# Gated attention and hash-routed experts in one kernel: expert blocks of three sizes instead of two

## The chip, the cores and the metric

The kernel runs on one core of a Trainium2 chip. The metric is the device time of one execution in microseconds. One more execution was recorded by the hardware profiler; all views below are of it.

## The reference

Eight sequences of 2496 tokens go through a gated attention unit with squared ReLU, and every token then through one of eight experts, which its token id alone selects.

```python
scores = (1.0 / S) * np.matmul(z, z.transpose(0, 2, 1))     # z: 8 x 2496 x 64
attn = np.maximum(scores, 0.0) ** 2
x = (u * np.matmul(attn, v)).reshape(B * S, D)              # u, v: 8 x 2496 x 256
expert_idx = token_ids * np.int64(2654435761) % np.int64(E) # 19968 tokens, E = 8
for e in range(E):
    mask = expert_idx == e
    out[mask] = np.maximum(x[mask] @ w1[e], 0.0) @ w2[e]    # w1: 256 x 1024, w2: 1024 x 256
```

All is float32.

## The kernel before

**Attention.** The kernel walks over 200 steps: 8 batches `b`, 5 groups of queries `g` (256 queries of each half of the sequence, the last group 224), and 5 groups of keys `s` in the order `STEPS[g]`. A step is called `i`, its place in its group `pos`. The product of the scores with v is done by a seven-product scheme over 2x2 halves (halves of the sequence and of the 256 columns of v), so `attend` (L310) makes 7 products of 2 matmuls into four PSUM banks, which `acc_ps` holds once. `score` (L228 to L250) makes the scores of a pair of groups two steps ahead (`AHEAD`), on PE, ACT (ReLU, square) and DVE. Because the scores are symmetric, a pair is computed once: `mirror` (L272, DVE) turns it, `keep` (L281, L285, SP) writes it to DRAM, and `recall` (L289, ACT's queue) reads it back for the other group. `sums` (L261 to L264, DVE) makes four differences of the scores for the products. After the last step of a group `join` (L320 to L328) combines the seven products from PSUM into `o`; the first product of the next group writes into the same banks, so it waits for that. z of the next batch is loaded in four chunks (`load_z`, L158), turned by DVE (`turn_z`, L171) and copied to the lower partitions (`copy_z`, L176).

**From attention to slots.** `places` runs a piece per step from step 5 on. It works out on DVE, from the token ids, which slot of `x_slots` (in DRAM) each token has: tokens of one expert stand together, in blocks. A finished group goes through `gate` (DVE transposes of `o`), `put` (L349, SP, to DRAM), `fetch` (L357, L361, SP, back with tokens on partitions, and u with it through `load_u`, L206), `multiply` by u (L374, DVE) and `sort` (L395, four indirect stores by POOL). Groups whose slots are not known yet are kept back in the list `waiting` and fetched once `places` is done. The last group of all has `gate_late` instead: PE transposes (L384) and a multiply straight from PSUM (L386). The last batch has its columns in such an order that the first two blocks (`SURE = 2`) hold no token of its last three groups.

**Experts.** A block of 512 tokens (`NL` = 32 of them) belongs to one expert. It uses the seven-product scheme too, on weights prepared in `w_dram`: `up_large` (L901) and `down_large` (L931). What is left over of each expert's tokens goes into `NR` = 35 blocks of 128 with plain products: `up_small` (L954), `down_small` (L965). The last of an expert's blocks may be filled up with empty slots. Seven products come from `products` in the order 1, 6, 7, 5, 2, 3, 4, with a `yield` behind each; product 2 adds into the PSUM tile of 1, and 3 into that of 5. Product 3 must wait until DVE has read 5 (L872). Products 1 and 5 have tiles with the tag "held", the others "other"; D has one tile of "other", U two.

The order of all instructions is written out by hand (`manual_schedule`). For block `i` the loop at the end runs parts that yield, in turns given by a string: U and u are the up products of the 512 block and of its small blocks, D and d the down products of the block before, X and x the turns of the next block's rows on DVE (`turn_x`, L697 to L705), G the late gate. U yields 14 times, D 7 times, X twice. Weights and rows are loaded on SP at the end of a block's turn, rows and w1 (L717) for the block after the next, w2 for the next.

```python
ORDER = {"": "UuUDUuUDUdUDU" "XUDXUDUxUDUUDU", ...
         "first": "UUUUGUUGUUUUUUUU", "second": "DUDUUDUUDUUDUU" "xXUuDUXUuDUxUU"}
for j in at(i + 2):
    load_x(j)
for m in range(2):
    for j in at(i + 2 - m)[:2]:
        load_w(j, m)
```

Of the kernel before, what the change touches and what calls it, by code (L numbers as in the profile page):

```python
# [25 lines left out]
def kernel(  # L26
# [19 lines left out]
    P = 128  # L46
# [6 lines left out]
    BLK = 512  # L53
    TB = BLK // P
    NL = -(-(N - E * (BLK - 1)) // BLK)
    NR = (N - NL * BLK + E * (P - 1)) // P
    NB = NL + NR
    NS = NL * TB + NR
# [254 lines left out]
    def join(g, acc, home):  # L313

        w = queries(g)
        p = {m: acc[k][:, half, 0:w] for m, (k, half) in BANK.items()}
        o = home.tile([P, DP, 2, W], F32, name="o")
        r = opool.tile([P, 2, W], F32, name="r", bufs=1)
        p1, u2 = r[:, 0, 0:w], r[:, 1, 0:w]
        nc.scalar.copy(p1, p[1])  # L320
        c = lambda i, q: o[:, i, q, 0:w]
        nc.vector.tensor_add(c(0, 0), p1, p[2])  # L322
        nc.vector.tensor_add(u2, p1, p[6])
        nc.vector.tensor_add(c(0, 1), u2, p[5])
        nc.vector.tensor_add(c(0, 1), c(0, 1), p[3])
        nc.vector.tensor_add(u2, u2, p[7])
        nc.vector.tensor_add(c(1, 1), u2, p[5])
        nc.vector.tensor_sub(c(1, 0), u2, p[4])  # L328
        return o
# [46 lines left out]
    def gate_late(b, g, o):  # L376

        x_sb = late.tile([P, 2, 2, D], F32, name="x_row")
        for q in range(2):
            ps = down_ps.tile([P, 2, D], F32, name="g_ps", tag="any")  # L380
            for t in range(2):
                m = keys(g, t)
                for i in range(DP):
                    nc.tensor.transpose(ps[0:m, t, ts(i, P)], o[:, i, q, ds(t * P, m)], ident[:])  # L384
                x, y = times_u(b, g, x_sb, q, t, m)
                nc.vector.tensor_mul(x, ps[0:m, t].rearrange("p (h i k) -> p i h k", h=DP, k=L), y)  # L386
                sort(b, g, x_sb, 2 * q + t)
            yield
# [26 lines left out]
    def places():  # L415

        with tc.tile_pool(name="route", bufs=1) as route:
# [31 lines left out]
            def fill():  # L449
                if unfilled:  # L450
# [3 lines left out]
                        x_dram[ds(NL * BLK + c * P, n * P), :].rearrange("(c p) d -> p c d", p=P), zero[:].unsqueeze(1).to_broadcast([P, n, D]))  # L454
# [59 lines left out]
            upto = wpool.tile([P, E, C], F32, name="upto", tag="w")  # L514
# [10 lines left out]
            nc.vector.tensor_tensor_scan(upto[:].rearrange(flat_e), one[:].to_broadcast([P, E * C]), upto[:].rearrange(flat_e), 0.0,  # L525
                                         op0=OP.mult, op1=OP.add)
            yield
            nc.vector.tensor_add(rank[:], rank[:], upto[:])
# [22 lines left out]
            large, large_end = share(count, BLK, 0, NL, "large")  # L551
            in_large = route.tile([P, E], F32)
            nc.vector.tensor_scalar(in_large[:], large[:], float(BLK), None, op0=OP.mult)
            nc.vector.tensor_sub(count[:], count[:], in_large[:])
            small, small_end = share(count, P, P - 1, NR, "small")
# [3 lines left out]
            shift = route.tile([P, E], F32)  # L559
            nc.vector.tensor_sub(shift[:], large_end[:], large[:])  # L560
            nc.vector.scalar_tensor_tensor(shift[:], shift[:], float(BLK), first[:], op0=OP.mult, op1=OP.subtract)
            more = route.tile([P, E], F32)
            nc.vector.tensor_sub(more[:], small_end[:], small[:])
            nc.vector.tensor_scalar(more[:], more[:], float(P), float(NL * BLK), op0=OP.mult, op1=OP.add)
            nc.vector.tensor_add(first[:], first[:], in_large[:])
            nc.vector.tensor_sub(more[:], more[:], first[:])
            nc.vector.tensor_sub(more[:], more[:], shift[:])

            for end, b0, nb in ((large_end, 0, NL), (small_end, NL, NR)):
# [4 lines left out]
                eb = route.tile([1, max(NL, NR)], F32, name="eb")  # L576
# [9 lines left out]
            past = upto  # L586
            nc.vector.tensor_tensor(past[:], rank[:], each(first), op=OP.is_ge)
            yield
            nc.vector.tensor_mul(past[:], past[:], each(more))
            yield  # L590
            nc.vector.tensor_add(rank[:], rank[:], each(shift))
            yield
            nc.vector.tensor_add(rank[:], rank[:], past[:])
# [79 lines left out]
    def large(j):  # L673
        return j < NL

    def slot_tiles(j):
        return range(j * TB, (j + 1) * TB) if large(j) else range(NL * (TB - 1) + j, NL * (TB - 1) + j + 1)

    def load_x(j):
        n = len(slot_tiles(j)) * P  # L680
        xq[j] = gpool.tile([P, n // L, DP, L], F32, name="xq" if large(j) else "xqs")
# [4 lines left out]
    def turn_x(j):  # L686

        n = len(slot_tiles(j))
        if large(j):
            x = gpool.tile([P, 2, DP, 2 * P], F32, name="xT")  # L690
            t = gpool.tile([P, 4, 2 * P], F32, name="xs")
# [3 lines left out]
        m = min(2, n) * P // L  # L695
# [12 lines left out]
    def turn_x_at_once(j):  # L708
        for _ in turn_x(j):
            pass  # L710

    def load_w(j, m):

        e = nc.sync.value_load(eb_i[0:1, j:j + 1], min_val=0, max_val=E - 1)
        if large(j):
# [43 lines left out]
    routed, is_routed = places(), False  # L759
# [13 lines left out]
    for i, (b, g, s) in enumerate(steps):  # L773
# [6 lines left out]
        if b + 1 < B:  # L780
            for after, do in ((0, load_z), (5, turn_z), (6, copy_z)):
# [6 lines left out]
        if i >= len(steps) - SURE:  # L788
            turn_x_at_once(i - len(steps) + SURE)
        if pos == NT - 1:  # L790
            done = (b, g, join(g, acc, opool if i < len(steps) - 1 else late))
# [8 lines left out]
        if pos == 0 and done is not None:  # L800
# [19 lines left out]
        elif is_routed:  # L820
# [6 lines left out]
            if len(fetched) < 2 and waiting and (len(waiting) > 1 or i > put_at + (1 if i < len(steps) - NT else 0)):  # L827
                fetched.append((i, fetch(*waiting.pop(0))))
        if is_routed and 0 <= i - 32 < C:
# [7 lines left out]
        if i == len(steps) - 2:  # L837
            load_u(b, g, late)
            load_w(1, 0)
# [46 lines left out]
    def up_large(j):  # L886
# [3 lines left out]
        h = hpool.tile([P, 2, 2, FQ, 2 * P], F32, name="h")  # L890
        sums = hpool.tile([P, 3, FQ, 2 * P], F32, name="hs")
        hid[j] = h, sums
        take = {1: (0, y11), 2: (2, y21), 3: (6, y22), 4: (3, t4), 5: (4, t1), 6: (5, t2), 7: (1, t3)}
        for f in range(0, FQ, 2):
            def made(m, ps):
                first = ps is None
                if first:
                    ps = up_ps.tile([P, 2, 2 * P], F32, name="h_ps", tag="held" if m in (1, 5) else "other")
# [5 lines left out]
            r = rpool.tile([P, 2, 2, 2 * P], F32, name="r")  # L904
# [12 lines left out]
    def down_large(j):  # L917
        h, sums = hid[j]
        x11, x12, x21, x22 = (h[:, k, i] for i in range(2) for k in range(2))
# [3 lines left out]
        def made(m, ps):  # L923
            first = ps is None
            if first:
                held = m in (1, 5)
                ps = down_ps.tile([P, 2, P], F32, name="o_ps", tag="held" if held else "other", bufs=2 if held else 1)
            x, k = take[m]
            for t in range(2):
# [4 lines left out]
        r = rpool.tile([P, 2, 2, P], F32, name="ro")  # L934
        o = rpool.tile([P, TB, D], F32, name="o_sb")
        c = lambda i, k: o[:, ts(i, 2), ts(k, P)]

        def done(x, i, k, ps=None):
            if ps is not None:
                nc.scalar.copy(x, ps)  # L940
            elif i != k:
                for t in (2 * i, 2 * i + 1):
# [19 lines left out]
    def down_small(j):  # L962
        ps = down_ps.tile([P, D], F32, name="o_ps", tag="any")
        for f in range(FP):
# [10 lines left out]

    ORDER = {"": "UuUDUuUDUdUDU" "XUDXUDUxUDUUDU", "made": "UuUDUuUDUdUDU" "XUDXuUDUxuUDUUDU",
             "next": "UuUDUuUDUdUDU" "XUDXUDUxUDUUxDU", "last": "UdUDUuUDUuUDU" "XUDXUDdUxUDUUDU",
             "first": "UUUUGUUGUUUUUUUU", "second": "DUDUUDUUDUUDUU" "xXUuDUXUuDUxUU"}
# [3 lines left out]
    SMALL = [range(0)] + [range(*(NL + (k * NR + NL // 2) // (NL - 1) for k in (i, i + 1))) for i in range(NL - 1)]  # L982
# [69 lines left out]
```

## Time and profile before

| what | us |
|---|---|
| timed runs | 2510.62, 2514.37, 2514.39 (median 2514.37) |
| the profiled execution | 2507.8 |
| its span (first to last instruction) | 2506.0 |
| attention (to the end of the last `attend`) | 1453.9 |
| experts (from there to the last matmul) | 1043.8 |
| after the last matmul | 8.3 |

Views of the trace have one group of instructions per line: start, length, engine, line of the source, operation, what is written and read, shape, count, and in brackets how long the engine was idle before it and what ended that. A float32 matmul has two records, so `x16` is eight matmuls. The mean clock granted to TensorE was 0.998. PE is TensorE, PEld its weight loads, DVE VectorE, ACT ScalarE, POOL GpSimd, SP SyncE; `SPq` and the like are their queues for DMA.

### The profile page before, as it was taken

Reading aid. Unit: us, or ns where it says so; the run is one execution under the profiler, and the core shown is the slowest. Engines: PE = TensorE matmul, PEld = TensorE weight load, DVE = VectorE, ACT = ScalarE, POOL = GpSimd, SP = SyncE. Lnnn points to the kernel's source line nnn. Section 1 sums busy time; section 2 is a strip of 40 time slices with the busy share of each in tenths; the row PEclk is TensorE's granted clock in tenths of the full one; section 3 lists DMA queues with packets and bytes.
Section 4 is the critical chain, followed back from the end, with each engine's and each line's share of the span. In section 5 each row is a group of like instructions: output and inputs, shape, how many; then the busy total and the mean of one; then the engine's idle time right before and its main releaser. Section 6 shows DMA issues by size and latency. Waiting matters only on the chain.

```text
span 2506.0 us, 36968 instructions
## 1 busy us (share of the span) xinstructions
PE 2476.4 (99%) x13631; PEld 2110.9 (84%) x13631; DVE 1653.4 (66%) x3151; ACT 705.8 (28%) x1203; POOL 548.9 (22%) x532
## 2 busy tenths in 40 slices
PE   8999999999999999999999989999999999999998
PEld 6787787787787777877787889999999999999998
DVE  7798768768778677687687665545555555555553
ACT  4324324224223233133233112222222222222221
POOL 0000333322332233233223221111111111111112
PEclk9999999999999999999999999999999999999999
DMA  8776899798797897897888797766676667667762
GB/s 148 201 206 176 244 272 227 211 248 203 234 262 191 244 249 184 251 250 198 246 244 230 200 284 240 244 227 227 236 236 203 222 225 232 204 224 245 236 217 72
DMA packets 604661, 557.19 MB, mean 222 GB/s; under 512 B 287068, under 2 KB 544685, under 8 KB 594240
## 3 DMA queue, kind: packets, MB, share of 16 engines
q1 hardware_dynamic: 513984, 369.74, 54.6%
q10 hardware_dynamic: 63168, 97.86, 11.9%
q0 software_dynamic: 27328, 87.23, 10.0%
q8 instruction: 107, 1.75, 0.3%
q14 instruction: 74, 0.61, 0.1%
HBM read 375.55 MB, written 175.60 MB: 220 GB/s over the span
## 4 chain that ended last, share of the span: by engine, by line
PE 91%; DMA 5%; DVE 2%; issue 1%; SPq 0%; ACT 0%; POOL 0%; POOLq 0%; DVEq 0%; ACTq 0%
PE acc L310 42%; PE o_ps L931 16%; PE h_ps L901 15%; PE s_ps L228 8%; PE h_ps L954 5%; PE o_ps L965 5%; DMA a<-scores 3%; DMA u_sb<-in_u_dram 1%; DMA scores<-mirror 0%; DMA zn<-in_z_dram 0%; DVE x_row L374 0%; DVE t L261 0%; DVE t L262 0%; DVE t L263 0%; ACT a L242 0%
## 5 line engine op out<-in xcount | busy, mean ns | idle before, releaser
L242 ACT ACTIVATE a<-s_ps 128x512 f32<-128x512 f32 (+2 forms) x508 | 248.1, 579 | 736.5 <-PE s_ps L228 697.5
L310 PE MATMUL acc<-t,vc 128*128 128x256 f32 (+3 forms) x1600 | 402.6, 374 | 0.0
L310 PEld LDWEIGHTS acc<-a,v_sb 128*128 128x128 f32 (+1 forms) x1600 | 293.3, 190 | 125.0 <-issue 45.5
L310 PE MATMUL acc<-a,v_sb 128*128 128x256 f32 (+3 forms) x1600 | 382.6, 382 | 5.3 <-DVE o L322 5.2
L395 POOL DMA_INDIRECT x_slots<-x_row,row x160 | 192.3, 1202 | 849.7 <-DVE x_row L374 642.9
L310 PE MATMUL acc<-t,v_sb 128*128 128x256 f32 (+3 forms) x1600 | 369.7, 373 | 0.0
L310 PEld LDWEIGHTS acc<-t,vc 128*128 128x128 f32 (+1 forms) x1600 | 303.0, 190 | 34.5
L310 PEld LDWEIGHTS acc<-t,v_sb 128*128 128x128 f32 (+1 forms) x1600 | 303.5, 190 | 33.6
L261 DVE TENSOR_TENSOR t<-a 128x512 f32<-128x512 f32 (+1 forms) x200 | 134.5, 672 | 226.5 <-ACT a L250 162.0
L901 PE MATMUL h_ps<-xs,w 128*128 128x256 f32 x1024 | 258.1, 380 | 0.0
L931 PEld LDWEIGHTS o_ps<-w,h 128*128 128x128 f32 x2048 | 248.6, 192 | 6.5
L228 PE MATMUL s_ps<-zT 64*128 64x512 f32 (+1 forms) x960 | 241.4, 617 | 9.1 <-DVE zT L171 8.4
L931 PE MATMUL o_ps<-w,h 128*128 128x128 f32 x2048 | 249.3, 275 | 0.0
L908 ACT ACTIVATE h<-h 128x512 f32<-128x512 f32 x192 | 121.0, 630 | 349.1 <-DVE h L872 153.2
L854 POOL DMA_INDIRECT out_dram<-o_sb,idx x128 | 126.7, 990 | 420.8 <-ACT h L908 271.2
L272 DVE STREAM_TRANSPOSE mirror<-a 128x512 f32<-128x512 f32 x320 | 198.4, 677 | 6.6 <-DMA scores<-mirror 6.5
L310 PE MATMUL acc<-a,vc 128*128 128x256 f32 (+3 forms) x800 | 201.1, 374 | 0.0
L901 PE MATMUL h_ps<-xT,w 128*128 128x256 f32 x768 | 194.0, 382 | 1.2 <-DVE h L872 1.2
L901 PEld LDWEIGHTS h_ps<-xs,w 128*128 128x128 f32 x1024 | 178.5, 191 | 15.5
L931 PEld LDWEIGHTS o_ps<-w,hs 128*128 128x128 f32 x1536 | 186.4, 192 | 4.8
L931 PE MATMUL o_ps<-w,hs 128*128 128x128 f32 x1536 | 187.1, 275 | 0.0
L611 POOL DMA_INDIRECT slot_tokens<-token,addr x160 | 169.7, 1061 | 49.0 <-issue 48.1
(154 smaller groups left out, 2756.7 us busy)
## 6 DMA issues: line engine op xcount, KB each, us to landing
w<-w_blocks SPq DMA_DIRECT2D x64, 1792.0 KB, 11.3
scores<-mirror SPq DMA_DIRECT2D x276, 256.0 KB, 4.8
a<-scores ACTq DMA_DIRECT2D x48, 1024.0 KB, 5.8
w1s<-in_moe_w_dram SPq DMA_DIRECT2D x35, 1024.0 KB, 10.3
w2s<-in_moe_w_dram SPq DMA_DIRECT2D x35, 1024.0 KB, 11.5
a<-scores ACTq DMA_DIRECT2D x32, 896.0 KB, 7.3
w_blocks<-w POOLq DMA_DIRECT2D x16, 1792.0 KB, 8.1
u_sb<-in_u_dram SPq DMA_DIRECT2D x72, 256.0 KB, 5.2
```

The lines of the kernel that those rows point to most:

```text
L228: nc.tensor.matmul(to, z_h[:, ds(h * HS + s * W + j * P, P)], at, start=True, stop=True)
L242: nc.scalar.activation(to, at, AF.Relu, scale=1.0 / S)
L261: nc.vector.tensor_sub(t1, y12, y11)
L272: nc.vector.transpose(m[:, :, j, h].rearrange("p (n i) k -> p i n k", i=QB), a[:, j, h].rearrange("p (i t) q r -> p i (t q) r", t=2))
L310: nc.tensor.matmul(acc[k][:, half, 0:w], x[0:n, j, :], y[0:n, j], start=(first and j == 0 and half == 0), stop=(last and j == 1), skip_gro ...
L395: st = nc.gpsimd.indirect_dma_start(out=x_dram[:, :], out_offset=bass.IndirectOffsetOnAxis(ap=row[0:m, c:c + 1], axis=0), in_=x_sb[0:m, q, ...
L611: st = nc.gpsimd.indirect_dma_start(out=slot_dram[:, None], out_offset=bass.IndirectOffsetOnAxis(ap=addr[0:n, to:to + 1], axis=0), in_=tok ...
L854: st = nc.gpsimd.indirect_dma_start(out=out[:], out_offset=bass.IndirectOffsetOnAxis(ap=idx[:, col:col + 1], axis=0), in_=o, in_offset=Non ...
L901: nc.tensor.matmul(ps[:, r], w1[j][:, k, ts(f + r, P)], y, start=first and r == 0, stop=True, skip_group_check=True)
L931: nc.tensor.matmul(ps[:, t], x[:, f, ts(t, P)], w2_block(w2[j], k)[:, f], start=first and t == 0 and f == 0, stop=f == FQ - 1, skip_group_ ...
L954: nc.tensor.matmul(ps[:, i, :], w1[j][:, c, ts(f + i, P)], x[:, 0, c, 0:P], start=(c == 0), stop=(c == DP - 1))
L965: nc.tensor.matmul(ps[:], hid[j][:, f], w2[j][:, f, :], start=(f == 0), stop=(f == FP - 1))
```

## The change

**Three sizes of block.** Between the 512 blocks and the 128 blocks there are now `NM` = 7 blocks of 256, always full, which use the same seven-product code on halves of 128 (`up_big`, `down_big`: U products 128 columns wide, D products half as many matmuls). `NR` falls from 35 to 21; the number of slots stays 163 x 128. `places` works with three levels instead of two, which makes it four steps longer. Every fifth block of the large ones is a 256 block; a small block goes with a 512 block, at most one each, none with a 256 block or with the first two; the last block has one, whose down product comes last of all.

**Order.** The turns X of the next block move: the first from the start of the second half of the string into the first half, ahead of D's second product, the second from behind one U and D to near the end. The special orders for two smalls go.

**Seam.** The last two groups now both use PE transposes (`gate_at_once`): all eight first, then the four multiplies. For group 3 of the last batch this stands at step 196 and replaces gate, put and fetch; its `join` writes `o` in another order of columns (`turned_back`). For the last group it stands in block 0, with both PSUM tiles at once, and its sorts come after block 0's products. The first two blocks' turns come at steps 197 and 198 instead of 198 and 199, u of group 3 is loaded at step 194 and u of the last group at 196 (before 197 and 198).

**Attention.** `load_z` comes two steps sooner. A fetch comes at the earliest four steps after the one before it.

```diff
+    BLK, MID = 512, 256
+    TB, TM = BLK // P, MID // P
     NL = -(-(N - E * (BLK - 1)) // BLK)
-    NR = (N - NL * BLK + E * (P - 1)) // P
+    NM = -(-(N - NL * BLK - E * (MID - 1)) // MID)
+    NR = (N - NL * BLK - NM * MID + E * (P - 1)) // P
...
+    def gate_at_once(b, g, o, x_sb, bank):
+        made = []
         for q in range(2):
-            ps = down_ps.tile([P, 2, D], F32, name="g_ps", tag="any")
+            made.append(bank())
+            for t in range(2):
+                for i in range(DP):
+                    nc.tensor.transpose(made[q][0:keys(g, t), t, ts(i, P)], o[:, i, q, ds(t * P, keys(g, t))], ident[:])
+        yield
+        for q in range(2):
             for t in range(2):
                 m = keys(g, t)
-                for i in range(DP):
-                    nc.tensor.transpose(ps[0:m, t, ts(i, P)], o[:, i, q, ds(t * P, m)], ident[:])
                 x, y = times_u(b, g, x_sb, q, t, m)
-                nc.vector.tensor_mul(x, ps[0:m, t].rearrange("p (h i k) -> p i h k", h=DP, k=L), y)
-                sort(b, g, x_sb, 2 * q + t)
-            yield
+                nc.vector.tensor_mul(x, made[q][0:m, t].rearrange("p (h i k) -> p i h k", h=DP, k=L), y)
...
-            past = upto
-            nc.vector.tensor_tensor(past[:], rank[:], each(first), op=OP.is_ge)
...
+            for past, (lowest, more, _) in ((past_mid, levels[1]), (upto, levels[2])):
+                nc.vector.tensor_tensor(past, rank[:], each(lowest), op=OP.is_ge)
+                yield
+                nc.vector.tensor_mul(past, past, each(more))
+                yield
...
-            for after, do in ((0, load_z), (5, turn_z), (6, copy_z)):
+            for after, do in ((-2, load_z), (5, turn_z), (6, copy_z)):
...
-        if i >= len(steps) - SURE:
-            turn_x_at_once(i - len(steps) + SURE)
+        if i == len(steps) - 4:
+            x_sb = rowpool.tile([P, 2, 2, D], F32, name="x_row", bufs=3)
+            for _ in gate_at_once(*done, x_sb, lambda: mm_ps.tile([P, 2, D], F32, name="g_ps", tag="mm")):
+                pass
+            to_sort += [(*done[:2], x_sb, k) for k in range(4)]
+        if 0 <= i - (len(steps) - 3) < SURE:
+            for _ in turn_x(i - (len(steps) - 3)):
+                pass
...
-            if len(fetched) < 2 and waiting and (len(waiting) > 1 or i > put_at + (1 if i < len(steps) - NT else 0)):
+            if len(fetched) < 2 and waiting and i >= fetch_at + 4 and (len(waiting) > 1 or i > put_at + 1):
                 fetched.append((i, fetch(*waiting.pop(0))))
+                fetch_at = i
...
         if i == len(steps) - 2:
-            load_u(b, g, late)
             load_w(1, 0)
+        if i == len(steps) - NT - 1:
+            load_u(b, g)
+        if i == len(steps) - 4:
+            load_u(b, g, late)
...
-    ORDER = {"": "UuUDUuUDUdUDU" "XUDXUDUxUDUUDU", "made": "UuUDUuUDUdUDU" "XUDXuUDUxuUDUUDU",
-             "next": "UuUDUuUDUdUDU" "XUDXUDUxUDUUxDU", "last": "UdUDUuUDUuUDU" "XUDXUDdUxUDUUDU",
-             "first": "UUUUGUUGUUUUUUUU", "second": "DUDUUDUUDUUDUU" "xXUuDUXUuDUxUU"}
+    ORDER = {"first": "UUUUGUUUGUUUUUUU", "second": "DUDUDUUDUUDUU" "XUxUDUXUDUUUU",
+             "other": "UuUDUuUXDUdUDU" "UDUDUxUDUXUDU", "end": "DDDDDDDd"}
...
+    for i in range(NBIG):
+        BIG.append(mid.pop(0) if i % (NBIG // NM) == NBIG // NM - 1 and mid else large.pop(0))
+        SMALL.append([])
+    for behind in (True, False):
+        for i in range(NBIG - 1, 1, -1):
+            if small and BIG[i] < NL and (BIG[i - 1] >= NL) == behind and (behind or i % 2 == 0 or len(small) == 1):
+                SMALL[i].append(small.pop())
```

## The prediction

> **What bounds the kernel now.** First the page's busy times, then its chain.
>
> ```profile
> PE 2476.4 (99%) x13631; PEld 2110.9 (84%) x13631; DVE 1653.4 (66%) x3151; ACT 705.8 (28%) x1203; POOL 548.9 (22%) x532
> ...
> PE 91%; DMA 5%; DVE 2%; issue 1%; SPq 0%; ACT 0%; POOL 0%; POOLq 0%; DVEq 0%; ACTq 0%
> ```
>
> TensorE is never far from busy, and the chain runs through it. Busy time of matmuls is modelled, so I took prices from starts in PE's timeline, here inside the expert blocks (start, length, group):
>
> ```profile
> 1579.52 3.62 PE L965 MATMUL o_ps<-w2s,h 128*128 128x256 f32 x16
> 1582.97 1.03 PE L901 MATMUL h_ps<-xT,w 128*128 128x256 f32 x4
> 1583.84 1.95 PE L931 MATMUL o_ps<-w,h 128*128 128x128 f32 x16
> 1585.62 1.03 PE L901 MATMUL h_ps<-xs,w 128*128 128x256 f32 x4
> ...
> 1589.14 1.95 PE L954 MATMUL h_ps<-xTs,w1s 128*128 128x128 f32 x16
> 1590.92 1.03 PE L901 MATMUL h_ps<-xs,w 128*128 128x256 f32 x4
> ```
>
> A group ends where the next starts. One matmul of the program is two records. So a U product of a 512 block (L901) costs 0.865 us, a D product (L931) 1.787, half a small up (L954) 1.785, a small down (L965) 3.45. A record with 128 columns costs 1.787/16 = 0.112, one with 256 0.216. Then PE in three stages (length, PE busy, PEld, DVE, ACT, POOL, clock, DMA share, GB/s):
>
> ```profile
> 1247.00:1427.00 180.00, 179.81 (x826) 141.97 (x822) 135.47 (x266) 57.52 (x95) 57.97 (x52) 1.00 0.83 228
> 1427.00:1462.00 35.00, 30.77 (x162) 29.71 (x158) 22.36 (x48) 3.33 (x7) 7.03 (x7) 1.00 0.90 230
> 1600.00:2480.00 880.00, 880.00 (x6006) 827.96 (x6005) 463.29 (x837) 209.41 (x387) 138.11 (x141) 1.00 0.67 221
> ```
>
> The expert stage has no gap at all in 880 us: only less PE work can shorten it. All of PE's idle time lies elsewhere; reading PE's timeline right through gives 8.4 us at the start, 0.68 in routing, 5.2 in eight places of attention, 7.1 at the seam, and 8.3 after the last matmul. The seam and one of the eight:
>
> ```profile
> 381.08 1.99 PE L310 MATMUL acc<-a,v_sb 128*128 128x256 f32 x8 [1.92 <-DVE o L322]
> ...
> 1453.93 1.03 PE L901 MATMUL h_ps<-xT,w 128*128 128x256 f32 x4
> 1462.48 0.51 PE L384 MATMUL g_ps<-ident,o 128*96 128x128 f32 x2 [4.71 <-DVE x_row L386]
> 1462.78 3.53 PE L901 MATMUL h_ps<-xT,w 128*128 128x256 f32 x8
> 1467.43 0.42 PE L384 MATMUL g_ps<-ident,o 128*96 128x128 f32 x2 [0.90 <-DVE x_row L386]
> 1474.21 1.13 PE L901 MATMUL h_ps<-xT,w 128*128 128x256 f32 x4 [1.18 <-DVE h L872]
> 1476.04 1.95 PE L931 MATMUL o_ps<-w,h 128*128 128x128 f32 x16
> ```
>
> **What the Trainium skill says.** "Perfetto Trace Analysis", Identifying the Most-Contended Engine: matmul occupancy is a poor measure of headroom, LDWEIGHTS busy a better one. The trace agrees: PEld is 828 of 880 us (94%) in the expert stage against 79% in attention (142 of 180), so no slack is hidden there. "TensorE: Matmul & The Clock Gate", Part 1: the HAM clock gate: after an idle window of about 3.4 us the array runs at half clock until it has been busy as long. The trace agrees: after 4.71 us of idling two products took 3.37 us (1462.78 to 1466.15) instead of 1.73; after 1.18 us none slowed. The same page's specification table: VectorE's queue is strictly first in, first out. Agreed: at 368 DVE sat 11.96 us for a<-scores, and the join (L322) that PE waited for at 381 stood behind. "DMA: Bandwidth & Descriptors", Issuing engines are not separate DMA queues: all queues share 16 engines. Agreed: SP's keeps (L281) waited 388.8 us for landings of ACT's a<-scores.
>
> **The change part by part.**
>
> *Blocks.* 32+35 blocks become 32 of 512, 7 of 256 and 21 of 128. A small costs 2x1.785+3.45 = 7.02 us of PE. A middle block has 14 U products of 4 records (0.447) and 7 D products of 8 (0.894): 6.26+6.26 = 12.5 us, where two smalls cost 14.0. Seven times 1.52: **-10.6 us**, all on the bounding engine. DMA falls too: 3.5 MB of weights for a middle block, 4 MB for two smalls. DVE gets more: 18 operations of about 0.42 us, 5 of 0.28 and a turn of 2.0, some 11 us, against 2.2 for two smalls; 62 us in a stage where DVE is 53% busy.
>
> *Turns (X) inside a block's sequence.* What they can delay is D's second product: its o_ps has one buffer, so D's third product waits until DVE has read the second, and X's two transposes (1.30 us) now stand ahead of that read. I walked each kind of cycle from the PE end of U's fourth product. Block 512 after a middle one: DVE's c22 ends at 0.2+0.69 = 0.89, X at 2.2, the read (0.28) at 2.5; PE arrives at 0.89+2x0.865 = 2.62. Fits by 0.1. Block 512 after 512: read done 2.62, PE at 3.52. Middle block after 512 without a small behind it (three cycles): DVE still has the previous block's sums, read done about 1.2+1.79, PE about 0.35 sooner. Near misses elsewhere: I take **+1.5 us** in all, bounds 0 and +8 (0.2 in each of 39 cycles). X needs its x rows landed: they are issued almost a cycle before (the turn at 1493.98 used loads issued at 1474.7; landing takes at most 16.9), so I cost this at nothing; the shortest cycle, 18.8 us, needs 5 MB of weights and rows, 13 us at the 390 to 450 GB/s seen after 1500. Were that cover gone, it would be the rival below.
>
> *Seam.* Group 3 of the last batch loses put, fetch and their SP issues; eight PE transposes at 0.224 come instead: +1.8. Its DVE multiplies need u, issued right behind u of group 2 (which ended DVE's wait at 1443); DVE reaches them at about 1446. The last group's transposes come at once in two buffers, so the waits of 4.71 and 0.90 and the half clock after the first (1.64) go. What is late next: the second half of block 0. From PE's end of U's seventh product DVE needs 0.9 for the subtraction, 1.5 for four multiplies, 2.5 for four sums, 2.26 up to c22: 7.2 us; PE arrives after 5x0.865 = 4.3. Stall 2.9 instead of 1.18, too short for the clock gate. From 1453.93 to the first D took 22.1; now 14x0.865+8x0.22+2.9 = 16.8. With +1.8, and the 0.34 us at 1494 gone: **-3.8 us**, bounds -6 and +2. The last sorts start about 9.5 us into the block, and their landing gates SP's x of block 2: landed near 28, turned at 33. w2 of block 0 waited for none of them (issued at 1457.9) and is due at 16.8: cover of about 2 us.
>
> *Attention.* Fetches: before, the backlog was drained in steps 24 to 39; now one every 4 steps from 28 to 104, then the same steps as before. Each moves a 0.5 MB x_row and 0.5 MB of u on SP. z: 8 issues a batch pass two steps of keeps, so the turns of z (DVE waited 32.8 us for zn, 11 times) have seven steps instead of five. The waits that reach PE total 5.2 us. They can vanish, or others come, since DMA is already 83 to 86% busy: I take **-2**, bounds -5 and +5. Routing is four steps longer (three more 1.45 us operations and some 20 short ones on DVE, 6 us); it lies in steps where DVE is 83% busy and PE lost 0.7 us; cost nothing, at worst +6.
>
> *End.* A small down now ends the program. Before, POOL still had four stores of 1.28 us after the last D. Now these lie beside the small's 3.45 us; copy 0.4, store 1.3, landing 3.9 follow, about 6.3 against 8.3. D's third product directly behind the second stalls 0.67. **-1.3**, bounds -2.5 and +1.
>
> Sum: -10.6+1.5-3.8-2-1.3 = **-16.2 us**. The profiled execution took 2507.8 (span 2506.0), below all three timed runs (median 2514.4); carried to the median: **2498.2 us**, 0.64% less. A measurement of this kernel tells about 0.2%, 5 us, from no change.
>
> **Rivals.**
> 1. *The moved turn sets D's pace* (slower than before). If the transposes wait for xq, or DVE's backlog is a little larger than walked, every cycle pays at D's third product. From 16.2/39 = 0.42 us a cycle (beyond my 1.5 us) the gain is gone; a full exposed turn, 1.3 us, would give +35: 2530. For it: margins of 0.1 us. Against: DVE 47% idle, x issued early. Chance 0.09 slower, 0.14 for a part of it (2502 to 2512).
> 2. *Attention pays for the fetches.* A backlog kept to step 104 puts x and u transfers beside recalls and mirrors in three batches instead of one. At +5 instead of -2: 2505. Chance 0.12.
> 3. *Everything hides.* No new stall among blocks, attention's waits gone: -10.6-4.5-5.2-1.5 = -22: 2492. Chance 0.12.
> 4. *The middle blocks do not pay*: if 128 columns cost a middle block's U more than L954's, say 0.6 instead of 0.447, 7x14x0.15 = 15 us are lost and the time stays about 2513. LDWEIGHTS at 94% speaks for it; L931 and L954 already run this shape at 0.112 a record, against it. Chance 0.03.
>
> My forecast has 0.5. Range 2489 to 2509: from rival 3 with a run's scatter to most of rivals 1 (part) and 2. Faster by over 0.2% 0.86, within 0.05, slower 0.09.
>
> **What would show it.** Right: L954's and L965's successors with 672 and 336 records; middle U products 0.45 us apart; PE without gaps among blocks except tenths of a us before D's third product; one gap of about 3 us at the seam, waiting for c22, at full clock; about 6 us after the last matmul. Wrong: repeated gaps of 0.4 us or more on h_ps or o_ps matmuls, DVE waiting for xq<-x_slots, PE waiting for w<-w_blocks, or joins late by more than 5 us in all.

## The result, and the profile after

| | before | after |
|---|---|---|
| median of 20 runs (lowest to highest), us | 2513.05 (2508.93 to 2516.10) | 2517.60 (2513.78 to 2524.72) |
| profiled execution; its span, us | 2507.8; 2506.0 | 2517.7; 2515.9 |
| mean granted clock of TensorE | 0.998 | 0.996 |
| start of block 0's first product | 1453.93 | 1477.80 |
| from there to the first D | 22.1 | 20.3 |
| from the first D to the last matmul's end | 1021.7 | 1011.7 |
| after the last matmul | 8.3 | 6.2 |

A matmul's end is taken here as the start of its last record plus the price of one. The ratio of the medians is 1.0024, with a 95% interval from 1.0016 to 1.0031: the change makes the kernel slower by 0.24%, where 0.64% less was forecast. The table already tells where. The experts and the end give 12.1 us, block 0 another 1.8, and attention takes 23.9. The three add up to the spans' difference of 9.9 to within a tenth.

The page of the kernel after, its busy times and its chain, answers the first two lines of the prediction:

```profile
PE 2477.2 (98%) x13751; PEld 2113.6 (84%) x13751; DVE 1715.0 (68%) x3346; ACT 724.0 (29%) x1259; POOL 556.7 (22%) x532
...
PE 85%; DMA 7%; DVE 4%; issue 2%; SPq 1%; ACT 0%; ACTq 0%; POOL 0%; POOLq 0%; another core or an unknown queue 0%; DVEq 0%
```

PE's busy time did not fall although the blocks need less of it, and its share of the chain fell from 91% to 85%: the chain now leaves PE for DMA, DVE and queues. Busy time hides this, because slowed matmuls count as busy too. The expert stage of the kernel after (stretch, length, then PE, PEld, DVE, ACT, POOL, clock, DMA share, GB/s):

```profile
1498.00:2510.00 1012.00, 1011.32 (x7114) 956.73 (x7112) 594.01 (x1148) 259.11 (x502) 162.16 (x162) 1.00 0.67 220
```

There is as little idle time among the blocks as before, and the stage ends 10 us sooner after its start. PE's timeline of the kernel after, at the seam, in a middle block and at the end:

```profile
1477.80 1.03 PE L929 MATMUL h_ps<-xT,w 128*128 128x256 f32 x4
...
1481.26 1.23 PE L386 MATMUL g_ps<-ident,o 128*128 128x128 f32 x8
...
1494.72 2.08 PE L929 MATMUL h_ps<-xT,w 128*128 128x256 f32 x4 [4.04 <-DVE h L899]
1496.59 1.64 PE L929 MATMUL h_ps<-xs,w 128*128 128x256 f32 x4
1498.07 1.95 PE L960 MATMUL o_ps<-w,h 128*128 128x128 f32 x16
...
1596.62 0.61 PE L929 MATMUL h_ps<-xs,w 128*128 128x128 f32 x4
1597.06 1.95 PE L960 MATMUL o_ps<-w,h 128*128 128x128 f32 x16
...
1608.17 1.05 PE L960 MATMUL o_ps<-w,h 128*128 128x128 f32 x8
1609.06 1.03 PE L929 MATMUL h_ps<-xs,w 128*128 128x256 f32 x4
...
2497.25 2.05 PE L960 MATMUL o_ps<-w,h 128*128 128x128 f32 x16 [0.58 <-DVE ro L893]
...
2506.28 3.62 PE L994 MATMUL o_ps<-w2s,h 128*128 128x256 f32 x16
```

A middle block's U product takes 0.44 us and its D product 0.89, as forecast (0.447 and 0.894). Eight transposes are eight records and take 1.06 us (1481.26 to 1482.32). The seam's long gap waits for c22 (what L899 finishes, and U's third product waits for), as forecast, but is 4.04 us and not 2.9, and half clock follows it: two products in 3.35 us.

Some of the gaps of attention in the kernel after:

```profile
169.65 3.01 PE L312 MATMUL acc<-a,v_sb 128*128 128x224 f32 x8 [2.13 <-DVE o L325]
...
318.36 1.99 PE L312 MATMUL acc<-a,v_sb 128*128 128x256 f32 x8 [2.04 <-issue]
...
380.25 4.27 PE L230 MATMUL s_ps<-zT 64*128 64x512 f32 x8 [4.04 <-ACT a L244]
...
1302.51 3.08 PE L312 MATMUL acc<-a,v_sb 128*128 128x256 f32 x8 [2.32 <-DVE o L325]
```

Most are first products of a group that wait for the join. In all, PE stands idle 18.2 us in 13 places of attention, where it was 5.2 in seven (the prediction counted eight). Slow matmuls come on top: 3.01 us for what takes 1.78, 4.27 and 3.08 for 1.99. By the profile's granted clock, 17.1 us of attention ran at half clock (3.41 us each from 170.03, 688.86 and 1303.26, and 6.83 from 378.25), and none of attention before (the first 13 us of each kernel apart); PE was busy for 15.1 of them, so they cost about 7.5 us. The 13.0 us of further idling, 7.5 of half clock and 1.1 of transposes make up 21.6 of the 23.9.

What DVE waited for before and after (engine, line, what it waited for: us in total, times, longest):

```profile
DVE t L261 <- DMA a<-scores: 52.7, 17, 12.0
DVE zT L171 <- DMA zn<-in_z_dram: 37.7, 11, 5.2
```

```profile
DVE t L263 <- DMA a<-scores: 96.4, 29, 15.0
...
DVE zT L173 <- DMA zn<-in_z_dram: 5.0, 2, 3.9
```

The wait for z went from 37.7 to 5.0 us, as an earlier load should do. But 43.7 us more of waiting for recalled scores came in its place (96.4 for 52.7). Waits of DVE reach PE only in small part: before, there were 90 us of these two, and PE was idle for 5.2.

### The profile page after: what moved, and what is told of

The parts are those of the page before. It is cut to its first block, busy times and chain, and to the rows that moved or that the text cites. A ratio compares the mean times of both kernels' runs of the same rounds, so it can differ in the third digit from the quotient of the medians.

```text
span 2515.9 us, 37295 instructions
## 1 busy us (share of the span) xinstructions
PE 2477.2 (98%) x13751; PEld 2113.6 (84%) x13751; DVE 1715.0 (68%) x3346; ACT 724.0 (29%) x1259; POOL 556.7 (22%) x532
## 3 DMA queue, kind: packets, MB, share of 16 engines
q10 hardware_dynamic: 63168, 97.86, 12.1%
## 4 chain that ended last, share of the span: by engine, by line
PE 85%; DMA 7%; DVE 4%; issue 2%; SPq 1%; ACT 0%; ACTq 0%; POOL 0%; POOLq 0%; another core or an unknown queue 0%; DVEq 0%
PE acc L312 37%; PE o_ps L960 17%; PE h_ps L929 17%; PE s_ps L230 8%; DMA a<-scores 4%; PE h_ps L983 3%; PE o_ps L994 3%; DMA scores<-mirror 2%; DMA u_sb<-in_u_dram 1%; DVE t L263 1%; DMA v_sb<-in_v_dram 1%; DVE t L265 1%; DVE t L264 1%; SPq L283 0%; ACT a L244 0%
## 5 line engine op out<-in xcount | busy, mean ns | idle before, releaser
L929 PE MATMUL h_ps<-xs,w 128*128 128x256 f32 (+1 forms) x1248 | 288.7, 361 | 0.1
L881 POOL DMA_INDIRECT out_dram<-o_sb,idx x142 | 143.4, 1010 | 630.9 <-issue 419.3
L960 PEld LDWEIGHTS o_ps<-w,h 128*128 128x128 f32 x2272 | 275.7, 192 | 7.8 <-DVE ro L893 1.1
L960 PE MATMUL o_ps<-w,h 128*128 128x128 f32 x2272 | 279.3, 275 | 0.6 <-DVE ro L893 0.6
L230 PE MATMUL s_ps<-zT 64*128 64x512 f32 (+1 forms) x960 | 245.7, 622 | 13.9 <-DVE zT L173 8.6
L936 ACT ACTIVATE h<-h 128x512 f32<-128x512 f32 (+1 forms) x234 | 138.6, 592 | 356.9 <-DVE h L899 138.3
L929 PEld LDWEIGHTS h_ps<-xs,w 128*128 128x128 f32 x1248 | 208.5, 191 | 17.0 <-issue 0.5
L929 PE MATMUL h_ps<-xT,w 128*128 128x256 f32 (+1 forms) x936 | 215.1, 362 | 4.4 <-DVE h L899 4.0
L960 PEld LDWEIGHTS o_ps<-w,hs 128*128 128x128 f32 x1704 | 206.9, 192 | 4.9
L960 PE MATMUL o_ps<-w,hs 128*128 128x128 f32 x1704 | 209.3, 275 | 0.0
L626 POOL DMA_INDIRECT slot_tokens<-token,addr x160 | 175.2, 1095 | 65.4 <-issue 47.5
```

The costliest lines, as they stand in the source:

```text
L230: nc.tensor.matmul(to, z_h[:, ds(h * HS + s * W + j * P, P)], at, start=True, stop=True)
L626: st = nc.gpsimd.indirect_dma_start(out=slot_dram[:, None], out_offset=bass.IndirectOffsetOnAxis(ap=addr[0:n, to:to + 1], axis=0), in_=tok ...
L881: st = nc.gpsimd.indirect_dma_start(out=out[:], out_offset=bass.IndirectOffsetOnAxis(ap=idx[:, col:col + 1], axis=0), in_=o, in_offset=Non ...
L929: nc.tensor.matmul(ps[:, r], w1[j][:, k, ts(f + r, P)], y, start=first and r == 0, stop=True, skip_group_check=True)
L936: lambda o, i, k, ps=None: nc.scalar.activation(o, o if ps is None else ps, AF.Relu))
L960: nc.tensor.matmul(ps[:, t], x[:, f, ts(t, P)], w2_block(w2[j], k)[:, f], start=first and t == 0 and f == 0, stop=f == FQ - 1, skip_group_ ...
```

## The experiments

Every kernel computes all of the result. Each ratio is against runs of the kernel before on the same chip. For the experiments the medians of these were 2510.25 (e1 to e4), 2512.21 (r1 to r3 and e5), 2508.56 (g1 to g3 and x1) and 2507.98 us (h1 to h4), so ratios are compared, not medians. A hundredth of a per cent is 0.25 us. "Attention" is the start of block 0's first product in the one profiled execution.

| kernel | ratio (95%) | attention, us |
|---|---|---|
| before | 1 | 1453.9 |
| after | 1.0024 (1.0016 to 1.0031) | 1477.8 |
| e1_after_z_back | 1.0023 (1.0012 to 1.0033) | 1473.9 |
| e2_after_fetch_back | 1.0000 (0.9990 to 1.0011) | 1472.1 |
| e3_after_both_back | 0.9995 (0.9987 to 1.0003) | 1469.8 |
| e4_before_z_sooner | 1.0032 (1.0016 to 1.0048) | 1461.4 |
| e5_before_fetch_4 | 1.0048 (1.0030 to 1.0065) | 1470.9 |
| r1_before_routing_at_9 | 1.0063 (1.0045 to 1.0081) | 1472.5 |
| r2_both_back_routing_at_1 | 0.9946 (0.9929 to 0.9962) | 1461.5 |
| r3_after_routing_at_1 | 1.0040 (1.0031 to 1.0050) | 1475.6 |
| g1_before_fetch_4_on_pool | 1.0028 (1.0018 to 1.0039) | 1455.7 |
| g2_routing_at_1_fetch_on_pool | 0.9922 (0.9908 to 0.9936) | 1450.0 |
| g3_after_fetch_on_pool | 0.9974 (0.9965 to 0.9984) | 1470.9 |
| x1_turns_together | 0.9999 (0.9991 to 1.0007) | 1456.4 |
| h1_z_back_fetch_on_pool | 0.9951 (0.9938 to 0.9965) | 1459.5 |
| h2_before_fetch_on_pool | 0.9970 (0.9958 to 0.9982) | 1447.9 |
| h3_before_routing_at_9_fetch_on_pool | 0.9993 (0.9985 to 1.0002) | 1457.1 |
| h4_before_z_sooner_fetch_on_pool | 1.0022 (1.0013 to 1.0031) | 1462.3 |

r2 and x1 have the same attention, and their single executions differ by 5.1 us there: the last column shows a direction, the ratios decide.

### Is it one of the two visible edits of attention?

The edits of z and of the fetches are undone in the kernel after, singly and together, and done alone in the kernel before.

```diff
# e1, e3 (after)                      e4 (before): the other way round
-            for after, do in ((-2, load_z), (5, turn_z), (6, copy_z)):
+            for after, do in ((0, load_z), (5, turn_z), (6, copy_z)):
# e2, e3 (after)
-            if len(fetched) < 2 and waiting and i >= fetch_at + 4 and (...):
+            if len(fetched) < 2 and waiting and (...):
# e5 (before)
+            if ... and (i >= fetch_at + 4 or i >= len(steps) - NT) and ...:
+                fetch_at = i
```

> The changed kernel with z loaded where it was before; all else stays changed. Attention of the changed kernel ends 23.9 us later than before (1477.8 against 1453.9), 0.9 of it the eight transposes. Theory Z (z loads two steps sooner push mirrors and recalls back): nearly all of the 23 us go, time 2495 to 2500, DVE's wait for a<-scores falls from 96 us to near 53. Theory F (fetches spread over steps 28 to 104): at most 5 us go, 2513 or more. Theory R (routing four steps longer, and the shift that comes with it): at most 5 us go as well.

> The changed kernel without the four steps between fetches; z stays sooner. Theory F: most of the 23 us go, 2495 to 2502, and the stalls at steps 40 to 100 vanish while the five after step 108 go with them only if they are echoes. Theory Z: stays at 2513 or above, with the stalls after step 108 (1.4, 1.0, 0.5, 2.3 us) still there. Theory R: stays.

> The changed kernel with both edits of attention undone: what is left are blocks, seam, end and longer routing. By the prediction's terms without attention: 10.0 (experts' first down product to the last matmul, as now measured), 2.1 (end), 1.8 (first block) less 0.9 (transposes): 13 us less than before, about 2500. Theories Z and F both expect that. Theory R expects the 4 us at step 20 and more behind it to stay: 2504 to 2510.

> The kernel before with only z two steps sooner. Theory Z: 10 to 20 us slower, 2523 or more, DVE's wait for zn near 5 us and for a<-scores near 90. Theories F and R: within 3 us of before, or faster by what the waits for zn cost.

> The kernel before with only the four steps between fetches (24 to 84). Theory F (the spread costs by itself): 5 to 8 us slower, 2516 to 2518, as its removal from the changed kernel gave 6 us. Theory R-shift alone: within 3 us of before.

Each edit alone costs in the kernel before: z 0.32% (8 us), the spread fetches 0.48% (12 us). In the kernel after, undoing z gives nothing (1.0023 for 1.0024), undoing the spread 6 us, undoing both 7. No single theory of the expectations holds: undoing z was to give back nearly all (Z), undoing the spread most of it (F). So both cost, but they do not add, and something else remains: with both undone, attention still ended 15.9 us late, some 12 us of it in steps 45 to 51. There PE waited 3.82 us at 390.07 for a copy of z, `zT<-zT`. The one edit of attention left was the longer `places`, for which the forecast had taken nothing.

### Is it the length of the routing?

`places` takes four steps more, so the groups kept back are fetched from step 28 on instead of 24. r1 delays it by four steps in the kernel before; r2 starts it four steps sooner in e3, and r3 in the kernel after.

```diff
# r1 (before)
-        if i >= 5 and not is_routed:
+        if i >= 9 and not is_routed:
# r2 (from e3), r3 (after)
-        if i >= 5 and not is_routed:
+        if i >= 1 and not is_routed:
```

> The kernel before with its routing started at step 9 instead of 5: the same pieces of work, so routing ends at step 27 as in the changed kernel and the kept back groups are fetched in steps 28 to 44 instead of 24 to 39. Theory R-shift (it is the later fetches, falling beside the recalls of batch 1's last group, that cost 10 us at steps 45 to 51 of the run with both edits undone): 8 to 12 us slower, 2518 to 2522, with the gaps at steps 45 to 51. Theory R-work (it is the third level's own work on DVE): within 2 us of before.

> The changed kernel with both edits of attention undone and routing started at step 1 instead of 5, so that it ends at step 23 and every fetch stands at the step where it stood before. Theory R-shift: the 10 us at steps 45 to 51 go, 2498 to 2500 against 2508.7 without this; the 2 us at the end of routing stay or move. Theory R-work: stays at 2507 to 2509.

> The changed kernel as it is, with routing started at step 1: the fetches every four steps run from 24 to 84 instead of 28 to 104. Theory R-shift alone: some 10 us less than the changed kernel, near 2505. If it is the spread itself (fetches at other places of a group than the third, beside mirrors and recalls) that costs: 2511 or more.

The delay alone costs the kernel before 0.63%, about 15 us, with not one operation added. Its step starts fall behind by 6.5 us in steps 13 to 26 and by 12 more in steps 45 to 51. Starting it sooner takes e3 from 0.9995 to 0.9946, about 12 us: this kernel has all of the change's blocks, seam and end, and its gain of 0.54% is near the 0.64% that was forecast. In the kernel after as a whole the same edit does not help: r3 is another 0.16% slower (1.0040), though the spread fetches now run from step 24 to 84 instead of 28 to 104. So the delay is not what costs where the fetches are spread; why r3 is slower still stays open.

What happened in steps 45 to 51 shows in SP's queue of r1 (start, length, queue, line, what is written and read, count), where the last two copies of z wait behind two fetches:

```profile
368.84 4.64 SPq L357 DMA_DIRECT2D x_row<-x  x1
374.15 8.48 SPq L206 DMA_DIRECT2D u_sb<-in_u_dram  x2
382.68 0.48 SPq L176 DMA_DIRECT2D zT<-zT  x1
383.33 0.46 SPq L357 DMA_DIRECT2D x_row<-x  x1
383.89 1.11 SPq L206 DMA_DIRECT2D u_sb<-in_u_dram  x2
385.10 3.98 SPq L349 DMA_DIRECT2D x<-x_sb  x4
389.52 0.68 SPq L176 DMA_DIRECT2D zT<-zT  x1
```

In the kernel before the same queue has:

```profile
368.72 0.99 SPq L176 DMA_DIRECT2D zT<-zT  x1
...
372.92 0.47 SPq L176 DMA_DIRECT2D zT<-zT  x1
```

The last copy comes at 389.52 instead of 372.92, of which only 7.5 us is the lag that r1 already had at step 44. DVE and PE of r1 then:

```profile
382.34 0.62 DVE L261 TENSOR_TENSOR t<-a 128x448 f32<-128x448 f32 x1 [13.15 <-DMA a<-scores]
```

```profile
394.14 3.75 PE L228 MATMUL s_ps<-zT 64*128 64x512 f32 x6 [5.05 <-DMA zT<-zT]
```

DVE waits 13.15 us for recalled scores, and PE 5.05 for z. Before, the last fetch of the backlog stood at step 39; now two fetches follow each other in steps 43 and 44, shortly before the change of batch, when the new batch's z is copied and its first scores are made.

### Is it the bytes, or SP's queue?

The bytes of x_row and u have to be moved in either case. In the next seven kernels the same transfers at the same steps are issued by POOL, and nothing else is changed; in h2, h3 and h4 the last fetch, which the seam waits for, stays on SP.

```diff
-            nc.sync.dma_start(out=x_sb[:]..., in_=xg_dram[b, g]...)
+            nc.gpsimd.dma_start(out=x_sb[:]..., in_=xg_dram[b, g]...)
-        load_u(b, g)
+        load_u(b, g, engine=nc.gpsimd)
```

> The kernel before with four steps between fetches (2524.4 measured, 12 us over before), and the fetch's transfers, x_row and u, issued by POOL instead of SP; same bytes at the same steps. Theory Queue (a fetch in the wrong step blocks SP: mirrors, z copies and puts behind it go late, and with them recalls): most of the 12 us go, 2510 to 2515. Theory Volume (it is the bytes beside the recalls on the shared DMA engines): 2520 to 2526 as on SP.

> The run with both edits of attention undone and routing from step 1 (2497.6), with the fetch's transfers issued by POOL. Theory Queue: the stalls left at steps 44 to 50 (4 us) and 70 shrink, 2491 to 2496. Theory Volume: within 3 us of 2497.6. A third possibility: POOL's own sorts, which wait for DVE, hold the fetch back, and DVE then waits for x_row: over 2500.

> The changed kernel as it is, with the fetch's transfers issued by POOL. Theory Queue: the 6 us that undoing the spread gave, and more, come back: 2500 to 2509. Theory Volume: 2515 to 2520, as the changed kernel.

> The changed kernel with the fetch's transfers issued by POOL and z loaded where it was before; fetches still every four steps from 28 to 104. With z two steps sooner the same kernel measured 2503.0 and kept five stalls of 2 to 4 us in attention. Theory Z2 (what is left of the loss is z's loads): the stalls at steps 70, 100, 125, 175 go, 2492 to 2497. Theory Spread (the later fetches cost even off SP): 2501 to 2505.

> The kernel before with the fetch's transfers issued by POOL, but for the very last fetch, which stays on SP. Baseline of the two that follow. Theory Queue: the 5 us of stalls in attention go, 3 to 6 us faster than before. Theory Volume: within 2 us of before.

> The kernel before with routing from step 9 (15 us slower than before: 6.5 at steps 13 to 26, 12.9 at steps 45 to 51, some given back later), and the fetches but the last issued by POOL. Theory Queue: the 12.9 us go and the 6.5 at routing stay, 5 to 8 us above the baseline without the shift. Theory Volume: 12 us or more above it.

> The kernel before with z two steps sooner (6.4 us slower than before when alone), and the fetches but the last issued by POOL. If z costs by meeting the fetches on SP: within 2 us of the baseline. If z's loads cost by themselves (they meet recalls and mirrors): 4 to 8 us above it, with stalls at the first step of batches.

| kernel | fetches on SP | fetches on POOL | difference in us |
|---|---|---|---|
| before | 1.0000 | 0.9970 | -7.5 |
| before, routing at 9 | 1.0063 | 0.9993 | -17.6 |
| before, z sooner | 1.0032 | 1.0022 | -2.5 |
| before, fetch every 4 | 1.0048 | 1.0028 | -5.0 |
| after | 1.0024 | 0.9974 | -12.6 |
| after, z back | 1.0023 | 0.9951 | -18.1 |
| both back, routing at 1 | 0.9946 | 0.9922 | -6.0 |

(The last column is the difference of the ratios times 2510; with the intervals of both ratios it is known to 3 to 5 us.) Four gain clear of that, "both back" just, and z sooner and the fetch every 4 lie within it. What goes with the queue shows best in h3, where the last two copies of z come at

```profile
361.90 0.75 SPq L176 DMA_DIRECT2D zT<-zT  x1
...
371.51 0.87 SPq L176 DMA_DIRECT2D zT<-zT  x1
```

instead of 382.68 and 389.52 in r1. The 12 us that r1 lost in steps 45 to 51 are gone: against h2, h3 falls behind by 0.7 us there.

g1's gain is larger than it seems, for on POOL its last fetch stands behind sorts, and the seam pays. PE of g1:

```profile
1471.95 0.66 PE L385 MATMUL g_ps<-ident,o 128*96 128x128 f32 x2 [12.46 <-DVE x_row L387]
```

Its attention ended at 1455.7 against 1470.9 for e5. The middle of attention, in the kernel before and in h2, which differ by the queue alone (columns as above):

```profile
500.00:1400.00 900.00, 896.67 (x4104) 708.70 (x4102) 672.72 (x1307) 286.20 (x470) 273.29 (x249) 1.00 0.85 230
```

```profile
500.00:1400.00 900.00, 900.00 (x4122) 712.75 (x4121) 676.56 (x1313) 288.95 (x474) 342.47 (x330) 1.00 0.84 231
```

The DMA share (0.85 and 0.84) and the rate (230 and 231 GB/s) are the same. PE was idle 3.33 us and is never idle now. In the kernel after the queue alone does not do that: PE is idle 9.95 us in this stretch and 12.09 in g3, which keeps the edits of z and of the fetches. "DMA: Bandwidth & Descriptors", Issuing engines are not separate DMA queues, says of several issuing engines that they will "only save the time on the sequencer". That agrees with the equal rate. (The 388.8 us that the prediction gave as agreement are waits of SP's queue for landings, and show no sharing.) But here the sequencer's time is what others stand behind: SP kept mirrors, puts and copies of z in line behind a fetch.

So the bytes alone are not the cost. What these runs do not separate is whether SP's order alone is, or also what comes with POOL: the same 557.19 MB are 604661 packets in the kernel before and 576149 in h2, and the fetches start at other times (those of steps 43 and 44 at 368.84 and 383.33 in r1, at 355.16 and 366.92 in h3).

Three costs outlive the queue.

**z two steps sooner.** h4 is 0.52%, 13 us, above h2; with the fetches on SP the edit cost 8, so fetches in SP's queue are not its cause. DVE's waits in h2, then in h4:

```profile
DVE t L262 <- DMA a<-scores: 46.5, 24, 7.6
DVE zT L171 <- DMA zn<-in_z_dram: 27.7, 12, 3.8
```

```profile
DVE t L262 <- DMA a<-scores: 85.1, 29, 8.3
DVE zT L171 <- DMA zn<-in_z_dram: 4.9, 2, 3.8
```

The 22.8 us less for z are paid with 38.6 more for scores, and these reach the joins. PE of h4, at the first step of a group:

```profile
315.79 3.67 PE L311 MATMUL acc<-a,v_sb 128*128 128x256 f32 x8 [3.68 <-DVE o L323]
```

Such gaps come four times (3.68, 2.64, 1.74, 2.72), one in each of four groups; h2 has none of them. Undone in g3, which is h1, the edit gives 0.23%, 6 us. That the loads of z hold up the mirrors behind them in SP's queue is my reading; no run shows it alone.

**The place of the routing's pieces.** h3 stays 0.23%, 6 us, above h2, most of it from a gap of 4.55 us at 135.08, with half clock around it, whose join stood on DVE behind a reduction of 1.48 us, among others. In the kernel after it is the `yield` that the third level adds: the piece with the small blocks' numbers comes one step later than before, on the last step of a group. DVE of the kernel before, and then of the kernel after:

```profile
159.67 0.18 DVE L580 TENSOR_SCALAR eb_i<-eb_i 1x67 int32<-1x67 int32 x1
...
166.52 0.41 DVE L322 TENSOR_TENSOR o<-r,acc 128x256 f32<-128x256 f32 x1
```

```profile
162.02 0.12 DVE L547 TENSOR_SCALAR small_i<-count 128x8 int32<-128x8 f32 x1
...
166.82 0.18 DVE L593 TENSOR_SCALAR eb_i<-eb_i 1x60 int32<-1x60 int32 x1
166.93 0.61 DVE L263 TENSOR_TENSOR t<-a 128x448 f32<-128x448 f32 x1
...
169.18 0.41 DVE L325 TENSOR_TENSOR o<-r,acc 128x256 f32<-128x256 f32 x1
```

The piece holds DVE from 162.02 to 166.93, then come the four differences, then the join (L325), without a pause; PE waits 2.13 us at 169.65 for it. Before, the piece was done at 159.85, and the join found nothing of it ahead. In r2, h1 and g2 a gap of the same size stays (1.97, 2.15 and 1.97 us).

**The spread fetches.** On POOL they leave one gap, 5.0 us at 534.52 in h1 and 5.21 at 531.26 in g1, against none there in g2 and h2. With the half clock behind it, g1's attention ends 7.8 us after h2's.

### Did the moved turns cost?

x1 is r2 with the turns X where the kernel before had them.

```diff
-             "other": "UuUDUuUXDUdUDU" "UDUDUxUDUXUDU", "end": "DDDDDDDd"}
+             "other": "UuUDUuUDUdUDU" "XUDXUDUxUDUUDU", "end": "DDDDDDDd"}
```

> The run with both edits of attention undone and routing from step 1 (2497.6), with the turns X put back to where they stood before in a block's sequence (the second half, one U and D apart). The prediction put 0 to 8 us of loss on the moved turns; the changed kernel's trace shows no gap among blocks, so all theories say within 2 us of 2497.6; if the old place does not suit middle blocks, gaps of tenths of a us per middle block, 2499 to 2503.

The ratio rises from 0.9946 to 0.9999, some 13 us, where 2 had been expected and 6 at worst. PE of x1, then DVE just before:

```profile
1600.89 1.13 PE L929 MATMUL h_ps<-xT,w 128*128 128x256 f32 x4 [1.75 <-DVE h L899]
```

```profile
1596.97 0.42 DVE L722 TENSOR_TENSOR xs<-xT 128x256 f32<-128x256 f32 x1
...
1598.10 0.42 DVE L725 TENSOR_TENSOR xs<-xs,xT 128x256 f32<-128x256 f32 x1
1598.44 0.68 DVE L893 TENSOR_TENSOR r<-r,h_ps 128x512 f32<-128x512 f32 x1
...
1600.15 0.69 DVE L899 TENSOR_TENSOR h<-h,h_ps 128x512 f32<-128x512 f32 x1
```

This gap comes seven times, 1.62 to 1.76 us each, 12.0 in all, once in the block behind each middle block: X's four subtractions stand ahead of the operations that lead to c22 (L899), and U's third product of the second half waits for that. The D products in between are those of the middle block and half as long, so PE arrives sooner; among 512 blocks the old order leaves no gap. With the turns moved there is no such gap.

## Why the prediction was wrong, step by step

**Blocks (-10.6) and moved turns (+1.5).** Right together: the stretch from the first D to the last matmul lost 10.0 us, where -10.6, +1.5, the 0.34 at 1494 and +0.67 at the end make -8.8. No gap appeared among the blocks, so the +1.5 was not needed, and rivals 1 and 4 are out. (Rival 1's full case was also added up wrongly: 35 us above the kernel before is 2549, not 2530.) The sign of the turns was misjudged: they are no cost of the change but what lets it pay. I had walked only the new order; walking the old one with a middle block would have shown it.

**Seam (-3.8).** Too good by about 3 us in this kernel: block 0 took 20.3 us instead of 16.8, although each set of eight transposes cost about 1 us and not 1.8. The term mis-sized is the stall, 4.04 us and 1.6 of half clock behind it for 2.9 without; 1.2 us of shorter pauses come before it. In g2 the stall is 2.50 and block 0 takes 17.05 us, near the forecast. Half clock follows there too, from 1464.31: 2.9 us was not too short for the clock gate. Why the kernel after is later there is not settled: DVE's c22 waited 1.27 us at 1493.98 for something that the trace does not name.

**End (-1.3).** The tail is 6.2 us (forecast 6.3) and D's third product stalls 0.58 (0.67).

**Attention (-2, bounds -5 and +5; routing at nothing, at worst +6).** This is the step that failed: 23.0 us lost beside the transposes, more than both upper bounds together. Four pieces of it:

- I counted on the earlier load to shorten DVE's waits for zn, 32.8 us, and with them PE's 5.2. Almost none of the 32.8 reached PE. It was slack, and with the load moved DVE waited longer for scores. Alone, the edit costs 8 us in the kernel before, and 13 with the fetches on POOL.
- I priced the fetches by bytes ("DMA is already 83 to 86% busy") and not by their place in SP's queue, although I had counted SP's issues. The spread alone costs 12 us.
- I priced the longer routing by its operations on DVE. What it also does is to start the fetches four steps later, which put the end of the backlog shortly before a change of batch: 12 of the 18.6 us that r1's attention lost in its profile. And a piece that stands ahead of a join is not hidden by DVE's mean of 83%.
- I priced no half clock behind the gaps that could come: about 7.5 of the 23 us, and the last section says after which gaps.

They overlap: by undoing alone one would find 0 for z and 6 us for the fetches, by doing alone 8, 12 and 15, of 23. Rival 2 named the fetches, but gave attention +5 us where it lost 23, and put it down to transfers beside recalls and mirrors, where the experiments point to the queue that issues them. The forecast's total would have been right without the three: g2 against h2, both with fetches on POOL, gains 0.48% (12.0 us), and their spans differ by 13.9, where blocks, turns, seam and end had been put at -14.2. That it fits so closely is in part luck: in these spans attention gives +2.1, block 0 -3.5, the other blocks -9.6 and the end -2.9.

**Best version.** g2, with the new blocks and seam, the old z and fetches, the routing from step 1 and the fetches on POOL, is 0.78% below the kernel before (0.64 to 0.92%). Of this 0.30% comes from moving the fetches to POOL, which the kernel before can do as well.

## What to carry to other kernels

A step that only waits may still be a slot in an order: before an earlier load or a spread transfer is booked as a gain, list what stands behind its issue in the same queue, and what of the wait reaches the engine that sets the time. When a stage of setup gets longer, follow the date of what its end releases, not its operations alone. And undo each part singly and together: parts can overlap, as the edits of attention do here, and one (here the turns) can be what another needs.

## What the runs showed of the hardware that I had not expected

**Short gaps can cost twice.** "TensorE: Matmul & The Clock Gate", Part 1: the HAM clock gate, led me to expect full speed after gaps under about 3.4 us of idling. Full gaps of 2.13, 1.97 and 2.32 us were followed by eight records in 3.01, 3.64 and 3.08 us instead of 1.78 to 2.00; others of the same size were not, as in e3, whose PE has

```profile
169.04 1.78 PE L312 MATMUL acc<-a,v_sb 128*128 128x224 f32 x8 [2.15 <-DVE o L325]
```

at the place of the gap at 169.65 in the kernel after. The page also calls the window free-running, and here the traces agree. In the kernel after half clock begins at 170.03, 378.25, 688.86 and 1303.26, which lie 61, 91 and 180 times 3.413 us apart. What decides is the idling inside one such window. Two windows of the kernel after, then two of e3 (columns as above; the first number behind the length is PE's busy time, and the clock stands third from the end):

```profile
166.62:170.03 3.41, 1.28 (x8) 0.56 (x5) 3.31 (x9) 2.93 (x9) 0.00 (x0) 1.00 0.48 74
170.03:173.44 3.41, 3.41 (x11) 3.09 (x10) 3.34 (x7) 0.00 (x0) 0.00 (x0) 0.50 0.66 249
```

```profile
164.97:168.38 3.41, 1.91 (x9) 0.69 (x8) 3.22 (x10) 2.17 (x9) 0.00 (x0) 1.00 0.82 160
168.38:171.79 3.41, 2.75 (x14) 2.62 (x15) 3.31 (x9) 0.76 (x1) 0.00 (x0) 1.00 0.81 269
```

The kernel after has its whole gap of 2.13 us in one window, and the next window runs at half clock. In e3 the end of a window cuts the gap into 1.50 and 0.65, and nothing slows. In the 18 traces, between 20 and 2475 us, all 43 windows at full clock with at least 1.94 us of idling were followed by half clock, none of the 58 with 1.00 to 1.85 us was, and two of the four in between were. So about 1.9 us of idling in a window is enough here, less than the whole idle window that the page names. A slowed window costs up to 1.7 us, half of its 3.41. For a forecast, a gap of 2 us in a busy stretch is worth 2 to 3.7 us, depending on where it falls.

**A transpose is one record.** Eight float32 transposes took 1.06 us, 0.13 each, where I had put two records of 0.112 to each as for a matmul.
